# Attention reads and a maxout layer on one core: the order of two groups of products in the read by the state rows

## The chip, the cores and the metric

The kernel runs on one core of a Trainium2 chip. The core has a matrix engine (TensorE, PE in the profile, with its weight loads as PEld), a vector engine (VectorE, DVE), an activation engine (ScalarE, ACT), a general engine (GpSimd, POOL) and a queue engine (SyncE, SP), which run at the same time and wait for each other by semaphores. The metric is the device time of one execution in microseconds; the median of five runs is compared.

## The reference, cut to what matters

Eight batches, each with 8 heads, 512 tokens x (64 wide) and 32 state rows. Tokens read from the state, the state rows read from the tokens, both by softmax attention; then a layer takes the largest of three products and multiplies it by an output matrix.

```python
scores  = scale * x @ state.T            # 512 x 32 for each batch and head
xread   = softmax(scores,  over state rows) @ state
sread   = softmax(scores.T, over tokens)    @ x      # the read by the state rows
rows = concat(xread, sread)              # 544 rows per batch, the heads side by side: 512 wide
h    = max(rows @ w1, rows @ w2, rows @ w3)          # 768 wide
out  = h @ w_out                                     # 512 wide, 4352 rows
```

In the read by the state rows, each state row needs two sums over the 512 tokens: of exp(score) times the token, and of exp(score) alone, by which the first is divided.

## The kernel before, in words

Layout. Numbers of type bf16 go into TensorE and fp32 sums come out in banks of PSUM, eight of them, taken in turn from one pool (`bank`, line 94). The 512 tokens of a batch stand as J = 4 blocks of 128 partitions; two heads make a pair, HP = 4 pairs. W holds w1 to w3, `sbd` the states of each head pair in block form.

Units of work. `scores` (line 231) makes exp of the scores of half a batch: 8 products into a bank `ps`, exp on ScalarE into `e`, sums and a reciprocal on VectorE, and a product on POOL into `a`. `a_crossbar` and `a_array` transpose `a` into `aT`, by a DMA and by TensorE. `m_unit` (line 179) multiplies states by weights, so that the scores `a` can meet states and weights in one step: 8 products into two banks `pm`, each on 64 rows and 32 columns of the array (line 184, with its place in the array given), then two copies into `M_sb`. `up` (line 286) makes one of the three products of a block of h (bank `pw`), `out_half` (line 308) half of an output block (bank `po`). All products go through `mm` (line 105), so that the profile puts them all on line 106; they are told apart by their tiles.

`state_reads` (line 264) is the read by the state rows. It takes one bank `pr`. In columns 0 to 255 (`psr`) it gathers the products with the tokens: for each of 4 head pairs and 4 token blocks a product of the whole array, with the tokens as weights and 64 columns of `e` (lines 269 to 272). In columns 256 to 383 (`pd`) it gathers the token sums of `e`: a weight of ones, 64 columns wide, placed in one half of the array's columns for even heads and in the other for odd heads, 128 columns of `e` for each of 4 token blocks (lines 274 to 277). VectorE then takes the reciprocal of `pd` (line 279) and multiplies the two halves of `psr` by it into `AT` (line 282). `AT` of all batches is the row block of the state rows, which `up` takes as a group of its own near the end.

Order. There is no planner: the instructions go to each engine's queue in the order in which the program issues them (`manual_schedule`, line 112). Three strings give it. OPENING (line 28) lists the units of the first batches one by one; `R 0`, `R 1` and `R 2` are their state reads. `R 0` stands behind transposes of tokens (`xT 1 0 a`) and ahead of scores, `R 1` behind an M unit (`M 0 0`), `R 2` behind an `up`. PERIOD (line 43) is one round of the steady part: `u` is `up`, `o` is `out_half`, `M` and `m` are M units, `S` scores, `P` and `L` the permuting and loading of later tokens, `X` the crossbar transpose of `a`, and `R` the state read of two batches ahead. In it R stands behind three M units and ahead of an `up`: `X u M m m R u o`. This gives the reads 3 to 7. LAST (line 46) is the round of the last token group and holds no R.

Of the kernel before, what the change touches and what calls it, by code (L numbers as in the profile page):

```python
# [51 lines left out]
def kernel(  # L52
# [22 lines left out]
    J = S // 128  # L75
    HP = H // 2
# [17 lines left out]
    def bank(shape, dt, name):  # L94
        return psum.tile(shape, dt, tag="bank", name=name)
# [9 lines left out]
    def mm(out_ap, lhsT, rhs, start, stop, pos=(0, 0)):  # L105
        nc.tensor.matmul(out_ap, lhsT, rhs, start=start, stop=stop, tile_position=pos)  # L106
# [87 lines left out]
    def tile_of(kind, b, pool, shape):  # L194
        if (kind, b) not in tiles:
            tiles[kind, b] = pool.tile(shape, BF16, tag=kind, name=kind)
        return tiles[kind, b]

    def x_nat(b):
        return tile_of("xn", b, xnp, [128, J, H, D])  # L200
# [4 lines left out]
    def e_of(b):  # L205
        return tile_of("e", b, att2, [128, J, 2, HP, Ns])
# [57 lines left out]
    def state_reads(b):  # L264
        e = e_of(b)
        pr = bank([128, 512], F32, "pr")
        psr = pr[:, 0:256].rearrange("p (hp a n) -> p hp a n", hp=HP, a=2)
        pd = pr[:, 256:384]
        for hp in range(HP):
            for j in range(J):  # L270
                mm(psr[:, hp, :, :], x_nat(b)[:, j, 2 * hp:2 * hp + 2, :], e[:, j, :, hp, :],
                   hp == 0 and j == 0, False)

        for j in range(J):
            for par in range(2):
                mm(pd[par * 64:par * 64 + 64], ones, e[:, j, par, :, :],
                   False, j == J - 1, pos=(0, par * 64))
        rd = att2.tile([128, HP, Ns], F32, tag="rd", name="rd")
        nc.vector.reciprocal(out=rd, in_=pd.rearrange("p (hp n) -> p hp n", hp=HP))  # L279
        for par in range(2):  # L280
            r = slice(par * 64, par * 64 + 64)
            nc.vector.tensor_mul(out=AT[r, :, b * Ns:(b + 1) * Ns],
                                 in0=psr[r, :, par, :], in1=rd[r])
# [64 lines left out]
    def issue(words):  # L348
# [7 lines left out]
        elif op_ == "sel":  # L356
            state_to_T()
        elif op_ == "lx":
            load_x(*n)
        elif op_ == "lw":  # L360
            load_w(*n)
        elif op_ == "lo":
            load_wout()
        elif op_ == "pm":
            permute_x(*n, eng)
        elif op_ == "xb":
            x_crossbar(*n)
        elif op_ == "xT":
            x_array(*n, eng)
        elif op_ == "S":  # L370
            scores(*n, eng)
        elif op_ == "R":
            state_reads(*n)
        elif op_ == "ab":
            a_crossbar(*n)
        elif op_ == "aT":
            a_array(*n, eng)
        elif op_ == "M":
            made.add(tuple(n))
            m_unit(*n, eng)  # L380
        elif op_ == "u":
            up(*n)
        else:
            out_half(*n, eng)
# [5 lines left out]
    for t in range(1, B):  # L390
        p, g = ORDER[t], ORDER[t + 1]
        nb = t + 2
        us = [(g, m, i) for m in range(MT) for i in range(3)]
        os = [(p, j, h) for j in range(J if p < B else ST // 128) for h in range(2)]
        sc = [0, 1]
        for what in (PERIOD if g != ORDER[-1] else LAST).split():
            if what == "u":
                up(*us.pop(0))
            elif what == "o":
                if os:  # L400
                    out_half(*os.pop(0), "a")
            elif what in ("M", "m"):
                if m_q:
                    m_unit(*m_q.pop(0), "aa" if what == "M" else "av")
            elif nb >= B:
                continue
            elif what == "S":
                scores(nb, sc.pop(0), "g")
            elif what == "P":
                if nb + 1 < B:  # L410
                    permute_x(nb + 1, None, "g")
                    x_crossbar(nb + 1)
            elif what == "L":
                if nb + 2 < B:
                    load_x(nb + 2)
            elif what == "R":
                state_reads(nb)
            elif what == "X":
                a_crossbar(nb)
# [32 lines left out]
```

The softmax here doesn't subtract the row's maximum and nothing guards it: scores larger than these inputs give would overflow.

## Time and profile before

| What | us |
|---|---|
| Median of 5 runs (lowest, highest) | 161.11 (160.5, 162.41) |
| The profiled execution's own time | 161.72 |
| Its span, first to last instruction | 159.9 |
| TensorE busy | 152.4 (95%) |
| VectorE busy | 112.1 (70%) |
| ScalarE busy | 94.7 (59%) |
| POOL busy | 44.2 (28%) |
| 128 token products of the read, 193 ns each | 5.2 |
| 64 sum products of the read, 225 ns each | 3.3 |
| 384 products of the M units, 327 ns each | 12.4 |
| 8 reciprocals of the read, 947 ns each | 7.6 |

The durations of products in the profile are longer than the time that each takes from the engine, since they overlap; the step from one start to the next tells what a product costs. A timeline line gives the start of a stretch of like instructions, its length to the end of the last, the engine, the line, the tiles written and read, and how many there are. In a form such as 64*32 the two numbers are the rows and the columns of the array that a product uses. An idle time and who ended it stand in brackets.

### The profile page before, as it was taken

How to read it: one execution, taken by the hardware profiler on the slowest of the kernel's cores; microseconds unless marked ns; L12 is line 12 of the kernel's file. 1: busy time of each engine (PE TensorE's matmuls, PEld its weight loads, DVE VectorE, ACT ScalarE, POOL GpSimd, SP SyncE). 2: the span in 40 equal slices, each digit the busy share in tenths (PEclk: the TensorE clock that was granted, in tenths of full speed). 3: DMA queues.
4: the chain of work that ended last, by engine and by line, in shares of the span. 5: the costliest groups of instructions: out<-in, count | busy, mean ns of one | idle time of the engine just before them, and what ended most of it. 6: DMA issues, size and time to landing. Idle time of an engine off the chain costs nothing.

```text
span 159.9 us, 3575 instructions
## 1 busy us (share of the span) xinstructions
PE 152.4 (95%) x1404; PEld 76.3 (48%) x1404; DVE 112.1 (70%) x200; ACT 94.7 (59%) x188; POOL 44.2 (28%) x48
## 2 busy tenths in 40 slices
PE   7988899979999999999999999999999999999991
PEld 2447453335456445544444444454445467654450
DVE  3266998858759969877886789688968844468701
ACT  3558978758474856595659565855686533344440
POOL 8915980092560650083009000500040000000000
PEclk9999999999999999999999999999999999999999
DMA  4999999949749679629972708470307033030254
GB/s 147 294 197 189 153 164 171 196 79 169 107 131 246 138 199 133 196 66 168 164 213 56 197 0 179 89 197 2 135 0 197 4 131 131 0 131 4 66 182 146
DMA packets 34400, 21.46 MB, mean 134 GB/s; under 512 B 19536, under 2 KB 31824, under 8 KB 34384
## 3 DMA queue, kind: packets, MB, share of 16 engines
q0 software_dynamic: 14400, 6.82, 33.7%
q1 hardware_dynamic: 19840, 14.29, 32.9%
q8 instruction: 11, 0.18, 0.4%
q10 hardware_dynamic: 144, 0.13, 0.2%
q14 instruction: 5, 0.04, 0.1%
HBM read 15.20 MB, written 8.91 MB: 151 GB/s over the span
## 4 chain that ended last, share of the span: by engine, by line
PE 79%; DMA 11%; POOL 4%; ACT 3%; DVE 1%; issue 1%; SPq 0%; POOLq 0%
PE pw L106 38%; PE po L106 28%; DMA x<-in_x_dram 11%; PE pm L106 4%; PE pr L106 3%; PE ps L106 2%; POOL a L246 2%; PE px L109 1%; ACT M_sb L101 1%; POOL xn L103 1%; PE pz L106 1%; ACT e L238 1%; ACT xn L101 1%; PE pa L109 1%; POOL x L153 1%
## 5 line engine op out<-in xcount | busy, mean ns | idle before, releaser
L106 PE MATMUL pw<-aT,M_sb 128*128 128x512 bf16 x288 | 71.9, 379 | 0.0
L106 PE MATMUL po<-wout,ht 128*128 128x512 bf16 (+1 forms) x210 | 52.4, 373 | 0.0
L304 DVE TENSOR_TENSOR t<-t,pw 128x512 bf16<-128x512 bf16 (+1 forms) x54 | 35.4, 656 | 19.6 <-PE pw L106 9.1
L300 ACT CAST t<-pw 128x512 bf16<-128x512 f32 (+1 forms) x54 | 30.6, 569 | 30.5 <-PE pw L106 29.6
L106 PEld LDWEIGHTS <-M_sb 128*128 128x128 bf16 x288 | 26.9, 98 | 31.6 <-issue 0.8
L306 DVE TENSOR_TENSOR ht<-t,pw 128x512 bf16<-128x512 bf16 (+1 forms) x54 | 35.2, 657 | 6.8 <-PE pw L106 3.0
L246 POOL TENSOR_TENSOR a<-e,rden 128x512 bf16<-128x512 bf16 x16 | 16.4, 1042 | 60.1 <-ACT e L238 36.6
L101 ACT CAST M_sb<-pm 128x384 bf16<-128x384 f32 x75 | 31.1, 507 | 1.2 <-PE pm L106 0.6
L106 PEld LDWEIGHTS <-ht 128*128 128x128 bf16 x210 | 19.6, 98 | 21.3 <-issue 1.9
L101 ACT COPY o<-po 128x512 f32<-128x512 f32 x32 | 18.8, 586 | 18.6 <-PE po L106 17.8
L103 POOL COPY xn<-x 128x2048 bf16<-128x2048 bf16 x6 | 11.3, 1887 | 8.9 <-DMA x<-in_x_dram 8.9
L106 PE MATMUL pm<-W,sbd 64*32 64x384 bf16 x384 | 12.4, 327 | 0.1
L242 DVE TENSOR_REDUCE den<-e 128x16 f32<-128x512 bf16 x16 | 10.6, 661 | 2.2 <-ACT e L238 2.1
L238 ACT ACTIVATE e<-ps 128x512 bf16<-128x512 f32 x16 | 8.9, 598 | 4.6 <-PE ps L106 4.6
L103 DVE CAST M_sb<-pm 128x384 bf16<-128x384 f32 x21 | 10.6, 534 | 0.0
L144 POOL DMA_DIRECT2D W<-in_moe_w_dram x12 | 9.0, 766 | 3.8 <-DMA x<-in_x_dram 3.2
L106 PE MATMUL pz<-zeros 128*128 128x512 bf16 x26 | 8.3, 478 | 1.2 <-DVE zeros L125 1.2
L106 PE MATMUL pw<-AT,W 128*128 128x256 bf16 x72 | 9.2, 273 | 0.0
L106 PEld LDWEIGHTS <-sbd 64*32 64x32 bf16 x384 | 4.3, 89 | 9.3 <-issue 8.7
L106 PEld LDWEIGHTS <-W 128*128 128x128 bf16 x72 | 7.0, 98 | 2.5
L279 DVE RECIPROCAL rd<-pr 128x128 f32<-128x128 f32 x8 | 7.6, 947 | 0.0
L153 POOL DMA_DIRECT2D x<-in_x_dram x7 | 6.6, 943 | 0.1
(39 smaller groups left out, 67.9 us busy)
## 6 DMA issues: line engine op xcount, KB each, us to landing
out_dram<-o SPq DMA_DIRECT2D x14, 512.0 KB, 2.9
x<-in_x_dram POOLq DMA_DIRECT2D x7, 512.0 KB, 7.9
W<-in_moe_w_dram POOLq DMA_DIRECT2D x6, 256.0 KB, 7.8
x<-in_x_dram SPq DMA_DIRECT2D x1, 1024.0 KB, 7.3
W<-in_moe_w_dram POOLq DMA_DIRECT2D x6, 128.0 KB, 10.7
wout<-in_moe_w_out_dram POOLq DMA_DIRECT2D x1, 768.0 KB, 13.5
out_dram<-o SPq DMA_DIRECT2D x3, 256.0 KB, 2.1
st<-in_state_dram SPq DMA_DIRECT2D x1, 512.0 KB, 3.7
```

The source lines that it names most:

```text
L101: nc.scalar.copy(out=o, in_=i)
L103: ENG[eng].tensor_copy(out=o, in_=i)
L106: nc.tensor.matmul(out_ap, lhsT, rhs, start=start, stop=stop, tile_position=pos)
L144: nc.gpsimd.dma_start(out=W[:, i, :, c], in_=w_v[i][:, :, c])
L153: nc.gpsimd.dma_start(out=x_sb[b].rearrange("p h j d -> p h (j d)"), in_=x[b].rearrange("h (p j) d -> p h (j d)", j=J))
L238: nc.scalar.activation(out=e.rearrange("p r n -> p (r n)"), in_=ps.rearrange("p j a hp n -> p (j a hp n)"), func=AF.Exp, scale=scale)
L242: nc.vector.reduce_sum(out=den, in_=e, axis=AX.X)
L246: ENG[eng].tensor_mul(out=a_of(b)[:, 2 * h:2 * h + 2].rearrange("p j a hp n -> p (j a hp) n"), in0=e, in1=rden.unsqueeze(2).to_broadcast(( ...
L279: nc.vector.reciprocal(out=rd, in_=pd.rearrange("p (hp n) -> p hp n", hp=HP))
L300: nc.scalar.copy(out=t[:, :nn], in_=pw[:, :nn])
L304: nc.vector.tensor_max(t[:, :nn], t0[:, :nn], pw[:, :nn])
L306: nc.vector.tensor_max(ht[:, m, :nn], tiles["t", g, m][:, :nn], pw[:, :nn])
```

## The change

The sum products come ahead of the token products. The mark that starts a bank afresh moves from the first token product to the first sum product of each column half; the mark that ends the group moves from the last sum products to the last token product. What follows on VectorE is issued as before, and the strings that give the order of the units are not touched.

```diff
         psr = pr[:, 0:256].rearrange("p (hp a n) -> p hp a n", hp=HP, a=2)
         pd = pr[:, 256:384]
+
+        for j in range(J):
+            for par in range(2):
+                mm(pd[par * 64:par * 64 + 64], ones, e[:, j, par, :, :],
+                   j == 0, False, pos=(0, par * 64))
         for hp in range(HP):
             for j in range(J):
                 mm(psr[:, hp, :, :], x_nat(b)[:, j, 2 * hp:2 * hp + 2, :], e[:, j, :, hp, :],
-                   hp == 0 and j == 0, False)
-
-        for j in range(J):
-            for par in range(2):
-                mm(pd[par * 64:par * 64 + 64], ones, e[:, j, par, :, :],
-                   False, j == J - 1, pos=(0, par * 64))
+                   False, hp == HP - 1 and j == J - 1)
```

## The prediction

> **What bounds the kernel now.** I read the page first (busy shares, slices, chain), then who waited for whom on TensorE alone, then TensorE's own timeline around every place where the changed function issues its products.
>
> From the page: the span, TensorE's share, its slices, its granted clock, and the chain of waits by engine.
>
> ```profile
> span 159.9 us, 3575 instructions
> PE 152.4 (95%) x1404; PEld 76.3 (48%) x1404; DVE 112.1 (70%) x200; ACT 94.7 (59%) x188; POOL 44.2 (28%) x48
> PE   7988899979999999999999999999999999999991
> PEclk9999999999999999999999999999999999999999
> ```
>
> The slices show a TensorE (PE) without holes from about 34 us to the end, at full clock. PE alone waited for little, and only early; this is the longest but one of its five waits, and the last in time:
>
> ```profile
> PE px L109 <- POOL xn L103: 0.9, 1, 0.9
> ```
>
> A busy PE row can hide gaps, because matmul ends are modelled. So I went by starts. After 34.6 us every pair of neighbouring 512-column products starts 215 to 216 ns apart, and up to 227 just after a stretch in smaller array tiles. Nothing waits there: each extra nanosecond in PE's stream lengthens the span, and each one taken out shortens it. These are the timeline's lines (start, length, engine, operation, tiles, count) for one regular round of the changed function, state rows' read 3 of 0 to 7:
>
> ```profile
> 58.70 0.59 PE L106 MATMUL pw<-aT,M_sb 128*128 128x512 bf16 x2
> 59.22 0.68 PE L106 MATMUL pm<-W,sbd 64*32 64x384 bf16 x24
> 59.84 0.64 PE L106 MATMUL pr<-e,xn 128*128 128x64 bf16 x16
> 60.41 0.41 PE L106 MATMUL pr<-e,ones 128*64 128x128 bf16 x8
> 60.76 0.61 PE L106 MATMUL pw<-aT,M_sb 128*128 128x512 bf16 x2
> 61.20 0.81 PE L106 MATMUL po<-wout,ht 128*128 128x512 bf16 x3
> ...
> 65.95 0.63 PE L106 MATMUL ps<-sbd,xT 128*128 128x64 bf16 x16
> 66.41 1.46 PE L106 MATMUL po<-wout,ht 128*128 128x512 bf16 x6
> ```
>
> The figures after the data type's counts say which part of the array is used: 128*128 is whole, 64*32 half the rows and a quarter of the columns, 128*64 half the columns. Compare lengths from start to next start. Sixteen whole-array products of 64 columns take 0.46 (65.95 to 66.41, whole before and after); the same sixteen in the read take 0.57, because the stretch is followed by a change of tile shape. The starts of single instructions give each change in ns, the same in every round:
>
> - whole to 64*32: 309 from the last 512-column start, against 216: 93 extra.
> - 64*32 to whole: 255 from the last M product's start in all 12 cases after 34 us; its 384 columns stream in 162 (the step from batch to batch): 93 extra, and the next product starts 11 late (40 against 29).
> - whole to 128*64: 123 against 29: 94 extra.
> - 128*64 to whole: 152 against 53 (step from pair to pair): 99 extra, and the next start 11 late (227 against 216).
>
> So a change of shape costs 93 to 110 ns of an engine with no slack.
>
> **The change part by part.** No instruction is added or removed: the same 16 token products and 8 sum products, weights, bytes, DMAs and evictions. The eight sums go in front; the start and stop flags move with them.
>
> *Rounds 3, 4, 5, 6, 7 (from 59.8, 75.6, 91.4, 107.1, 122.9 us), M units before, a whole-array product behind.* Before, from the last M start (59.582) to the second pw start (60.982): 255 to the first token product, 448 to the last, 123 to the first sum, 195 to the last, 152 to pw, 227 to the second pw: 1400 ns. Three changes of shape. After: X to the first sum, 195, 152 to the first token product (taken from sums to pw), 448, then 29 to pw (whole to whole, as from ps to po) and 216: 1040 + X.
>
> X, M unit to sums, 64*32 straight to 128*64, is in no trace row. From below: 162, if two column-tiled shapes need no emptying between them. From above: 162 + 2 x 94 = 350, if rows and columns are paid for as two changes. The nearest rows are 64*32 to whole (93 extra) and whole to 128*64 (94 extra): every change seen costs about 94, whatever it changes, so X = 255. Then 1295, a gain of 105 ns a round; with X = 162 it is 198, with X = 350 it is 10. A rule of the Trainium skill (TensorEngine Tiling (Array Packing), "Key Properties") weighs against the larger gain: a switch of mode, unlike a switch of tile within a mode, empties the array. By the rule X keeps its 93 and the gain is 105 x 5 = 0.53 us; by hope it is 198 x 5 = 0.99 us. The trace shows the emptying for each of four switches and no switch between two tiled modes; I side with the rule.
>
> *Round 1 (22.1 us), also behind an M unit.* Same 105 ns, but PE then runs into the wait of 0.93 us for the permuted tokens:
>
> ```profile
> 31.85 1.47 PE L106 MATMUL pw<-aT,M_sb 128*128 128x512 bf16 x6
> 34.24 0.62 PE L109 MATMUL px<-ident,xn 128*128 128x128 bf16 x8 [0.93 <-POOL xn L103]
> ```
>
> That wait hangs on a load issued from POOL's queue at 21.67 and landed at 32.25, which came after POOL's multiply at 19.74, not after the read. So it is hidden; without that cover it would be another 0.1.
>
> *Round 2 (48.0 us).* Whole-array products stand on both sides:
>
> ```profile
> 47.10 1.03 PE L106 MATMUL pw<-aT,M_sb 128*128 128x512 bf16 x4
> 47.96 0.63 PE L106 MATMUL pr<-e,xn 128*128 128x64 bf16 x16
> 48.52 0.41 PE L106 MATMUL pr<-e,ones 128*64 128x128 bf16 x8
> 48.87 1.47 PE L106 MATMUL pw<-aT,M_sb 128*128 128x512 bf16 x6
> ```
>
> Two changes before, two after: zero.
>
> *Round 0 (13.6 us).* Transposes before it, scores behind it, both whole: zero too. It waits for the second half of e (its third product starts at 13.831, 181 ns after the second); the sums of tokens 0 and 1 now stand ahead of that wait. Worked out, the last token product starts near 14.5. The scores behind wait until 14.74 for ScalarE's copy of xT (13.67, 1.02 long), so up to 0.24 us either way is covered.
>
> *VectorE.* The reciprocal needs only the sums, which now end 0.5 us earlier. That buys nothing where it counts:
>
> ```profile
> 59.94 1.01 DVE L103 CAST M_sb<-pm 128x384 bf16<-128x384 f32 x2
> 60.87 0.95 DVE L279 RECIPROCAL rd<-pr 128x128 f32<-128x128 f32 x1
> 61.86 0.59 DVE L282 TENSOR_TENSOR AT<-pr,rd 64x128 bf16<-64x128 f32 x2
> ```
>
> VectorE is in the M units' casts until then: from the second cast (60.403) to the reciprocal (60.868) is 465 ns, the same as from cast to cast (467). A second rule speaks against an earlier start: the skill's page PSUM — Partial Sum Buffer, "PSUM bank collisions raise a hardware error", wants a reader kept off a bank that TensorE still writes, by bank and not by address. Sums and token products share bank pr. By the rule the reciprocal is released by the last token product, which ends at 60.825 in the new order (59.582 + 255 + 195 + 152 + 448 ns, and 193 for itself); by the trace it is released by the last sum, 60.822. Either way 60.87 stands: zero. Queued behind it on VectorE are the two AT multiplies, which now wait for the token products (done a whole microsecond before 61.86), and the maxima; AT is read by PE only at 127.73, and round 7 writes it by 125.52.
>
> *Banks.* Bank pr and those after it are reached 0.1 us sooner at most. Taking the bank pool in order, pr follows a pw read out 0.71 us before, and the later ones have 0.3 us or more. The tightest, an M unit's bank 30 ns behind ScalarE's copy of po (59.53 against 59.558), stands ahead of the read and moves with PE. No queue of SP or POOL is crossed by the moved instructions.
>
> Sum: 5 x 0.105 = 0.53 us. Profiled execution: 161.72, of which 159.9 is span and 1.8 lies around it; after, span 159.4 and 161.2. The median of the runs, 161.11, lies 0.6 below that execution; the same gain from it gives 160.6.
>
> **The rivals.**
>
> - *Free between tiled shapes.* X = 162: 161.11 - 0.99 = 160.1. For it: sums and M units both split the columns. Against: row split differs, and every switch seen cost 93 or more.
> - *It gains nothing:* the switch away from M to sums costs as two, X = 350: 5 x 0.01, so 161.1. For it: rows and columns change together. Against: from 64*32 to whole both change too, for 93.
> - *Slower: M to sums is a dear switch.* Place: between the last M product and the first sum, five times. All eight 64*32 tiles must be through before half-column weights come in, and a sum needs both row halves. Price: X - 360 per round. It decides from X = 360; a whole per cent (1.61 us) needs X = 682, an extra of 520 where the dearest switch in the trace costs 110. At X = 500 it gives 161.8.
>
> **How the numbers follow.** Chances: forecast 0.70, free switch 0.12, no gain 0.10, slower 0.08. The forecast's time is 160.6. Range 159.9 to 161.3: from the free switch to the two-change price, each widened by 0.2 for the median of runs that spread over 1.9 us (160.5 to 162.41). About 1% either way is what a measurement of this kernel can tell from no change; every case but the far end of the dear switch lies inside it. Above 1% faster asks for 0.32 us a round, about all that its three switches cost together, so only scatter gets there: 0.05. Slower by over 1%: 0.05.
>
> **What would show it.** In PE's timeline the sums start 0.62 after an M stretch of 24 products (last M start to first sum 255 ns), token products follow 0.35 later, and pw 0.47 after those; from the first M start to po is 1.87 instead of 1.98. Round 2 keeps its length, the wait before px grows to about 1.0, and the reciprocal still follows the cast at 465 ns. Wrong if the step from M to sums is not near 255, if a gap opens in PE after 34 us, or if the transposed a lands late: it was issued at 72.27, landed at 79.72 beside a token load, and is used at 80.4, so 0.7 us is all it has.

## The result, and the profile after

The changed kernel takes 160.34 us (median of 43 runs) where the kernel before, run beside it, takes 160.88 (80 runs). The ratio is 0.9972, with a 95% interval from 0.9956 to 0.9987: 0.45 us faster, between 0.2 and 0.7. The ratio leaves out the runs that are more than 1.5% above the fastest of their kernel, which the medians include. The forecast was 160.6, half a microsecond under the 161.11 known then.

The profiled execution took 160.78 us with a span of 159.0, against 161.72 and 159.9. The page of the changed kernel, span, busy shares and TensorE's slices:

```profile
span 159.0 us, 3575 instructions
PE 150.7 (95%) x1404; PEld 75.3 (47%) x1404; DVE 112.0 (70%) x200; ACT 94.7 (60%) x188; POOL 44.2 (28%) x48
PE   6878899979999999999999999999999999999991
```

The span is 0.9 shorter, and only part of that is the change. TensorE's timeline of the changed kernel (start, length, engine, operation, tiles, count):

```profile
12.38 1.06 PE L109 MATMUL px<-ident,xn 128*128 128x128 bf16 x16
13.36 0.42 PE L106 MATMUL pr<-e,ones 128*64 128x128 bf16 x8
...
21.49 0.36 PE L106 MATMUL pm<-W,sbd 64*32 64x384 bf16 x8
21.77 0.41 PE L106 MATMUL pr<-e,ones 128*64 128x128 bf16 x8
22.12 0.64 PE L106 MATMUL pr<-e,xn 128*128 128x64 bf16 x16
...
33.84 0.62 PE L109 MATMUL px<-ident,xn 128*128 128x128 bf16 x8 [0.98 <-POOL xn L103]
...
46.69 1.03 PE L106 MATMUL pw<-aT,M_sb 128*128 128x512 bf16 x4
47.65 0.41 PE L106 MATMUL pr<-e,ones 128*64 128x128 bf16 x8
48.00 0.64 PE L106 MATMUL pr<-e,xn 128*128 128x64 bf16 x16
48.47 1.46 PE L106 MATMUL pw<-aT,M_sb 128*128 128x512 bf16 x6
...
58.82 0.68 PE L106 MATMUL pm<-W,sbd 64*32 64x384 bf16 x24
59.43 0.41 PE L106 MATMUL pr<-e,ones 128*64 128x128 bf16 x8
59.77 0.64 PE L106 MATMUL pr<-e,xn 128*128 128x64 bf16 x16
60.25 0.60 PE L106 MATMUL pw<-aT,M_sb 128*128 128x512 bf16 x2
60.68 0.81 PE L106 MATMUL po<-wout,ht 128*128 128x512 bf16 x3
```

Round 3, from the first M start to po, is now 60.68 - 58.82 = 1.86 where it was 1.98; read 2 (47.65 down to 48.47, with the step ahead of it) keeps its length.

The px line at 33.84 is the boundary that matters for reading the two spans: its start hangs on a load of tokens. In the profile of before that load was issued at 21.67 and landed at 32.25, and px began at 34.24; in this one it was issued at 21.31 and landed at 31.84, and px began at 33.84. So 0.41 of the 0.93 by which the spans differ (159.935 and 159.002 unrounded) lies ahead of px. It isn't the change's: TensorE was 0.35 ahead already in the transposes in front of read 0, where nothing changed had run yet. They start at 12.38 here, and in the profile of before at 12.73:

```profile
12.73 1.06 PE L109 MATMUL px<-ident,xn 128*128 128x128 bf16 x16
```

The load's own time was shorter by another 0.05. From px at 33.84 (34.24 before) to the start of the last product, single starts give 121.967 us before and 121.437 after: the change itself is 0.530 us. Behind that, the two take 3.72 and 3.73.

### The profile page after: what moved, and what is told of

Its sections match the earlier page's. It is cut to its first block, busy times and chain, and to the rows that moved or that the text cites. A ratio compares the mean times of both kernels' runs of the same rounds, so it can differ in the third digit from the quotient of the medians.

```text
span 159.0 us, 3575 instructions
## 1 busy us (share of the span) xinstructions
PE 150.7 (95%) x1404; PEld 75.3 (47%) x1404; DVE 112.0 (70%) x200; ACT 94.7 (60%) x188; POOL 44.2 (28%) x48
## 4 chain that ended last, share of the span: by engine, by line
PE 79%; DMA 11%; POOL 4%; ACT 3%; DVE 1%; issue 1%; SPq 0%; POOLq 0%
PE pw L106 38%; PE po L106 28%; DMA x<-in_x_dram 11%; PE pm L106 4%; PE pr L106 3%; PE ps L106 2%; POOL a L246 2%; PE px L109 1%; ACT M_sb L101 1%; POOL xn L103 1%; PE pz L106 1%; ACT e L238 1%; ACT xn L101 1%; PE pa L109 1%; POOL x L153 1%
## 5 line engine op out<-in xcount | busy, mean ns | idle before, releaser
L242 DVE TENSOR_REDUCE den<-e 128x16 f32<-128x512 bf16 x16 | 10.6, 661 | 2.1 <-ACT e L238 2.1
L103 DVE CAST M_sb<-pm 128x384 bf16<-128x384 f32 x21 | 10.6, 534 | 0.0
L106 PE MATMUL pz<-zeros 128*128 128x512 bf16 x26 | 7.6, 448 | 1.2 <-DVE zeros L125 1.2
```

Of the source, the lines that this page charges most:

```text
L103: ENG[eng].tensor_copy(out=o, in_=i)
L242: nc.vector.reduce_sum(out=den, in_=e, axis=AX.X)
```

## The experiments

In what follows "the main stretch" is that stretch, from the first px after the wait for the permuted tokens to the start of TensorE's last product: it is free of the scatter ahead of px and good to some nanoseconds (121.437, 121.437 and 121.436 in three profiles whose reads 3 to 7 are as in the change), while the ratio of a run carries 0.0015 to 0.004 of uncertainty. Reads 0 and 1 lie ahead of it.

**Which reads give the gain.** Two kernels, each with the new order in some reads only: `b >= 3` in the first, `b < 3` in the second. `sums` and `tokens` issue the two groups of products; their two flags are the marks that start the bank and end the group.

```diff
...
+        if b >= 3:
+            sums(pd, e, True, False)
+            tokens(b, psr, e, False, True)
+        else:
+            tokens(b, psr, e, True, False)
+            sums(pd, e, False, True)
...
```

> New order in reads 3 to 7 only, reads 0 to 2 as before. Theory (one change of array shape less behind the M units, five times, 0.11 us each): the whole gain, ratio to before 0.9966, that is 160.3 where before gives 160.9; M to sums 252 ns, as in the changed kernel. Rival (part of the gain comes from the opening, where the changed kernel's profiled execution was already 0.4 us ahead by read 3): less than half of it, ratio 0.998 to 0.999.

> New order in reads 0 to 2 only, reads 3 to 7 as before. Theory: nothing, ratio 1.000; read 1 gains 0.11 us and loses it in the wait for the permuted tokens, which ends at the same distance from the load. Rival (the opening gives part): ratio 0.998 or lower.

With reads 3 to 7 alone: ratio 0.9983 (0.9948 to 1.0018), main stretch 121.437, the same to the nanosecond as in the changed kernel. With reads 0 to 2 alone: ratio 0.9993 (0.9969 to 1.0017), main stretch 121.968, that of before. The intervals of the ratios cannot part the two; the main stretches do. They show that reads 3 to 7 give the whole 0.530 and that read 2 gives nothing; reads 0 and 1 have to be looked at where they stand. In the second kernel, read 1 did become shorter (from the last start before it to the second product behind it, 1302 ns against 1409), and its place and the wait behind it look like this in TensorE's timeline:

```profile
21.76 0.35 PE L106 MATMUL pm<-W,sbd 64*32 64x384 bf16 x8
22.04 0.41 PE L106 MATMUL pr<-e,ones 128*64 128x128 bf16 x8
22.39 0.64 PE L106 MATMUL pr<-e,xn 128*128 128x64 bf16 x16
22.87 2.32 PE L106 MATMUL pw<-aT,M_sb 128*128 128x512 bf16 x10
...
33.89 0.62 PE L109 MATMUL px<-ident,xn 128*128 128x128 bf16 x8 [0.76 <-POOL xn L103]
```

TensorE still waits 0.76 us for the tokens, whose load landed at 31.89, 2.00 us before px. In all ten profiles with such a wait, px starts 2.00 us behind the landing. So the gain of read 1 goes into that wait.

**Is it the place next to the M units, or the sums being ready sooner?** The read moves one product unit on.

```diff
-... X u M m m R u o u u u o u u
+... X u M m m u R o u u u o u u
```

> The changed kernel with the read of the steady rounds one product unit later (u R instead of R u behind the three M units), so that whole-array products stand on both sides of it. Theory (the gain lies in the place next to the M units): three changes of shape again, the time of before, ratio 1.000, 160.9. Rival (the gain lies in the sums being ready earlier, for VectorE): the gain stays, ratio 0.997.

The ratio is 1.0014 (0.9987 to 1.0041), the main stretch 121.971, 4 ns from that of before. The gain is gone, with the sums first all the same and the marks of the bank where the change puts them. TensorE's timeline shows where it went:

```profile
58.36 0.68 PE L106 MATMUL pm<-W,sbd 64*32 64x384 bf16 x24
58.97 0.61 PE L106 MATMUL pw<-aT,M_sb 128*128 128x512 bf16 x2
59.51 0.41 PE L106 MATMUL pr<-e,ones 128*64 128x128 bf16 x8
59.85 0.64 PE L106 MATMUL pr<-e,xn 128*128 128x64 bf16 x16
60.33 0.81 PE L106 MATMUL po<-wout,ht 128*128 128x512 bf16 x3
```

The two pw products take 0.54 to the next start instead of 0.43: out of the M shape and into the half columns again. The same kernel answers what releases the reciprocal, since VectorE is free before it here. VectorE's timeline:

```profile
59.07 1.01 DVE L103 CAST M_sb<-pm 128x384 bf16<-128x384 f32 x2
60.53 0.96 DVE L279 RECIPROCAL rd<-pr 128x128 f32<-128x128 f32 x1 [0.45 <-PE pr L106]
```

The sums were done by 59.92 (last start 59.70, 0.22 long), the last token product at 60.49. The reciprocal starts at 60.53: it waits for the last product into the bank, although it reads only the sums. So putting the sums first gives VectorE nothing, not even where it has the time. Whether it is the bank that it waits for, the tile `pr` or the product with the mark that ends the group, the runs don't tell: here the three end together.

**Is a change between two column-split shapes cheaper?** The sums go into four column quarters, the split that the M units have, so that the two differ in rows alone.

```diff
-            for par in range(2):
-                mm(pd[par * 64:par * 64 + 64], ones, e[:, j, par, :, :],
-                   j == 0, False, pos=(0, par * 64))
+            for q in range(4):
+                mm(pd[q * 32:q * 32 + 32], ones[:, 0:32], e[:, j, q // 2, :, :],
+                   j == 0, False, pos=(0, q * 32))
```

> The changed kernel with the sums in four column quarters (16 products of 32 weight columns, four at a time) instead of two halves, so that M units and sums share the column split and differ in the row split alone. Theory (any change of shape empties the array): step from the last M start to the first sum stays near 252 ns, time as the changed kernel, ratio to before 0.997. Rival (a change between shapes with one column split is free): that step falls to about 162 ns, five times 0.09 us, ratio 0.994.

Ratio 0.9988 (0.9963 to 1.0013), main stretch 121.390. The step from the last M start to the first sum is 252 or 253 ns in the five rounds, as with halves. TensorE's timeline, to be set beside the changed kernel's 0.61 and 0.34:

```profile
58.54 0.68 PE L106 MATMUL pm<-W,sbd 64*32 64x384 bf16 x24
59.15 0.41 PE L106 MATMUL pr<-e,ones 128*32 128x128 bf16 x16
59.49 0.64 PE L106 MATMUL pr<-e,xn 128*128 128x64 bf16 x16
```

A change in the rows alone costs as much as one in both. Between places of one shape it is otherwise: from one quarter to the next the step is 3 or 4 ns. Sixteen sum products in quarters take as long as eight in halves, even 8 ns less a read.

**Is the number of changes what is paid?** The sums of two token blocks ahead of the token products, those of the other two behind.

```diff
...
+        sums(pd, e, True, False, range(0, 2))
+        tokens(b, psr, e, False, False)
+        sums(pd, e, False, True, range(2, 4))
...
```

> The sums split: those of two token blocks ahead of the 16 token products, those of the other two behind them; the same products, two more changes of shape than the changed kernel has. Theory: one way into half columns and out again costs 94 + 24 + 99 + 11 = about 0.23 us a read; reads 3 to 7 and read 2 pay it, so 1.3 us more than the changed kernel and 0.75 us more than before: ratio to before 1.005, from the wait for the permuted tokens to the last product 122.7 us against 121.97 before. Rival (the number of changes is not what is paid, only the step behind the M units): as the changed kernel, 121.4 us and ratio 0.997.

Ratio 1.0043 (1.0014 to 1.0071), main stretch 122.788: 1.35 us above the changed kernel where 1.3 was expected, 0.82 above before where 0.75 was. TensorE's timeline:

```profile
57.86 0.68 PE L106 MATMUL pm<-W,sbd 64*32 64x384 bf16 x24
58.47 0.30 PE L106 MATMUL pr<-e,ones 128*64 128x128 bf16 x4
58.71 0.64 PE L106 MATMUL pr<-e,xn 128*128 128x64 bf16 x16
59.28 0.30 PE L106 MATMUL pr<-e,ones 128*64 128x128 bf16 x4
59.51 0.61 PE L106 MATMUL pw<-aT,M_sb 128*128 128x512 bf16 x2
59.95 0.81 PE L106 MATMUL po<-wout,ht 128*128 128x512 bf16 x3
```

From 57.86 to 59.95 is 2.09, against 1.86 in the changed kernel: 0.23 for two more changes, with the same products.

**What fewer sum products bring.** If TensorE has no slack, then work taken from it should come off the span. POOL adds the four token blocks of `e` into `es` (`ef` is `e` as one row), and in reads 3 to 7 two sum products are left of eight.

```diff
...
+            nc.gpsimd.tensor_add(out=e2, in0=ef[:, 0:512], in1=ef[:, 512:1024])
...
+            nc.gpsimd.tensor_add(out=es.rearrange("p a hp n -> p (a hp n)"),
+                                 in0=e2[:, 0:256], in1=e2[:, 256:512])
...
+        summed = tile_of("es", b, att2, [128, 2, HP, Ns]).unsqueeze(1) if b >= 3 else e
-        for j in range(J):
+        for j in range(1 if b >= 3 else J):
             for par in range(2):
-                mm(pd[par * 64:par * 64 + 64], ones, e[:, j, par, :, :],
+                mm(pd[par * 64:par * 64 + 64], ones, summed[:, j, par, :, :],
...
```

> The changed kernel, with POOL adding the four token blocks of e beforehand in reads 3 to 7 (two additions in bf16, after its products for a), so that two sum products are left instead of eight. Theory (PE has no slack after 34 us): the stretch of sums shrinks from 195 to about 5 ns, 0.19 us a read, 0.95 us in all: from the wait for the permuted tokens to the last product 120.5 us against 121.4 in the changed kernel, ratio to before 0.991. Rival (POOL's 1.6 us a read hold back its copy of the tokens and its load, or slow VectorE, and PE waits): a gap in PE's row, ratio 0.997 or higher.

The main stretch fell to 120.596, by 0.84. TensorE's timeline of the read:

```profile
58.58 0.68 PE L106 MATMUL pm<-W,sbd 64*32 64x384 bf16 x24
59.19 0.25 PE L106 MATMUL pr<-es,ones 128*64 128x128 bf16 x2
59.37 0.64 PE L106 MATMUL pr<-e,xn 128*128 128x64 bf16 x16
```

The step from the last sum to the first token product is 176 ns here, 24 more than behind eight sums, hence not 0.95. Yet the ratio was 0.9993 (0.9954 to 1.0031). TensorE did not wait anywhere in the main stretch; the gain was lost behind its last product, where the span went on for 4.5 us instead of 3.7. Three kernels on one chip were to tell why, the third with one edit more:

```diff
-    op = ctx.enter_context(tc.tile_pool(name="op", bufs=2))
+    op = ctx.enter_context(tc.tile_pool(name="op", bufs=3))
```

> The changed kernel once more, as the measure for the two beside it. From the wait for the permuted tokens to the last product 121.44 us as in its first profile, ratio to before 0.997.

> The kernel with the presummed e once more. Its first profile had TensorE 0.84 us ahead of the changed kernel, and lost 0.8 us of that behind TensorE's last token group: the state rows' last writes took 2.7 to 3.4 us instead of 1.7, and ScalarE's copy of a block o waited 1.6 us for its buffer. If that was one execution's accident: tail from the last product's start to the end 3.7 us, ratio 0.992. If it belongs to this kernel: tail 4.5 us again, ratio 0.997 or above.

> The presummed kernel with three buffers for o instead of two, so that no copy of o waits for the write of the block two before. If the wait for that buffer is what loses the gain: tail 3.7 us, ratio 0.992. If the slow writes themselves set the end: the tail stays 4.5 us.

| Kernel | ratio to before (interval) | main stretch | from the last product's start to the end |
|---|---|---|---|
| changed | 0.9958 (0.9933 to 0.9982) | 121.436 | 3.73 |
| presummed | 0.9996 (0.9970 to 1.0023) | 120.597 | 4.99 |
| presummed, three o | 0.9934 (0.9908 to 0.9960) | 120.597 | 3.73 |

It was no accident. The timeline of the presummed kernel's end (issues of the SP queue as SPq):

```profile
148.85 1.73 SPq L350 DMA_DIRECT2D out_dram<-o  x4
...
150.82 0.59 ACT L101 COPY o<-po 128x512 f32<-128x512 f32 x1 [0.71 <-PE po L106]
...
153.51 0.59 ACT L101 COPY o<-po 128x512 f32<-128x512 f32 x1 [2.10 <-DMA out_dram<-o]
153.99 0.38 ACT L101 COPY oh<-po 128x256 f32<-128x256 f32 x1
```

and of the one with three buffers:

```profile
150.22 1.73 SPq L350 DMA_DIRECT2D out_dram<-o  x4
...
152.19 0.59 ACT L101 COPY o<-po 128x512 f32<-128x512 f32 x1 [0.71 <-PE po L106]
153.49 0.59 ACT L101 COPY o<-po 128x512 f32<-128x512 f32 x1 [0.71 <-PE po L106]
154.14 0.37 ACT L101 COPY oh<-po 128x256 f32<-128x256 f32 x1
```

The four writes of the state rows' last block, 64 KB each, land 3.2 to 3.8 us after issue in the first and 3.0 to 3.7 in the second, against 1.6 to 1.7 in the changed kernel. With two buffers ScalarE's copy waits 2.1 us for them; with three it doesn't, and the end follows TensorE again. So the wait for the buffer is what lost the gain: shown. Why the writes are slow there is only argued: a 16 KB load of instructions falls on them (started at 150.62 and 151.89 in the two kernels, at 145.27 in the changed kernel, which has more TensorE instructions ahead of that point). The traces speak for it. In all ten profiles where such a load meets writes of the state rows, early ones or the last four, the first of them to land does so 1.0 to 1.2 us after the load's end, wherever that falls. The kernel with the quarters has no load there, and all its writes of the state rows take 1.6 to 1.7. But no run moved the load alone.

The version with three buffers has the lowest median on that chip, 159.65 us against 159.90 for the changed kernel and 160.41 for before. Its interval overlaps that of the changed kernel, so its lead over that one rests on the main stretch and the tail of one profile each, not on the runs. What three buffers alone do to the changed kernel wasn't tried; its trace shows no wait for one.

## Why the prediction was right, point by point

- *A change of shape is what is saved, one in each of rounds 3 to 7.* Right. The five rounds went from between 1397 and 1400 ns to 1292 or 1293; 1295 was worked out. The term X, M unit to sums, was set at 255 between ends of 162 and 350; it measured 252 or 253. (LAST does hold an R in its string, other than said above; no batch is left for it by then, so it issues nothing and the rounds are five.)
- *The rule that a switch of mode empties the array* (the Trainium skill, TensorEngine Tiling (Array Packing), "Key Properties"). The page names no price; the 93 came from the trace. The trace of before showed no switch between two tiled modes; the changed kernel and the quarters show two such, both 252, which is 90 more than the 162 that the M product streams. Both agree with the rule, though the emptying itself is no row of a trace, and the rival of a free switch has fallen. So have "no gain" and the dear switch, which needed 350 and more than 360 in turn.
- *Round 2: zero.* 1350 before, 1349 after. *Round 0: covered.* From the last transpose ahead of it to the second product of the scores behind it, 1214 before and 1213 after.
- *Round 1: hidden in the wait before px.* Right for these profiles, where the wait grew from 0.93 to 0.98 (by less than the 0.11 that read 1 gained, since the load took 0.05 less). But that cover is not a constant: over all profiles it was between 0 and 1.0 us, as the load landed between 30.5 and 32.3. In the second profile of the presummed kernel, which has the new order in read 1, the wait was 0.04; by an estimate from these numbers, with the old order TensorE would have come 0.07 too late there, and so much of read 1's gain counts in such an execution. The prediction took one execution's wait for the kernel's.
- *VectorE: zero.* Right, the reciprocal followed the start of the second cast by 464 ns, as VectorE's timeline of the changed kernel has it:

```profile
59.53 1.02 DVE L103 CAST M_sb<-pm 128x384 bf16<-128x384 f32 x2
60.46 0.95 DVE L279 RECIPROCAL rd<-pr 128x128 f32<-128x128 f32 x1
```

The last token product ended at 60.42, 0.05 ahead of the reciprocal, so this trace can't tell whether the casts or the bank held it. The kernel with the read one unit on, where VectorE is free, settles the choice that was left open: the reciprocal is released with the bank's last product, and not with the last sum.
- *The sum.* 0.525 us by the working, 0.530 in the main stretch, 0.45 (0.2 to 0.7) by the ratio, 0.54 between the medians. The runs alone exclude the 0.99 of a free switch and the 0.05 of no gain; that it is 0.53 comes from the main stretch. The 160.6 stands 0.26 above the measured 160.34 mostly for another reason than the change: it was taken off 161.11, the median of five runs, and the kernel before has 160.88 over 80. The profiled execution fell by 0.94, of which 0.41 was scatter ahead of px; had only the two profiled times been compared, the gain would have looked nearly twice its size.

## What to carry to other kernels

Where a tuned kernel keeps TensorE without a gap, cost an edit by the steps from start to start, not by busy times: five 0.1 us pieces could be summed blind to within 0.01, and the same steps told that three of eight places would give nothing (one of them only as long as a wait covers it). Order small-tile products so that unlike tile shapes touch and whole-array work lies together, but count the changes on both sides of each place first; the same edit one unit further on is worth nothing. And a gain on the bounding engine is only kept if what ends the kernel follows it: look at the buffers and writes behind the last product before trusting the sum.

## What the runs showed that was not expected

A reader of one part of a PSUM bank was held until the last product into the whole bank, 0.57 us after the part that it reads was done; the prediction had left that open. Two kernels whose instruction counts differ slightly had their last 64 KB writes at 1.7 and at up to 3.8 us. And the start of the main stretch moved by 1.7 us between profiles of kernels that are the same up to there or nearly so (32.5 to 34.2), 2.00 us after one load had landed in all but the split sums, where TensorE came 0.11 later than that. Up to 0.8 of it is there before the first read begins (12.9 to 13.7), up to 1.1 is the time of that load (9.5 to 10.6): the whole is larger than all the effects studied here.
